# A planned attention and MLP kernel: attention work with new inputs yields to MLP blocks on TensorE, other VectorE durations in the planner, another order at the start

## The chip, the core and the metric

The kernel runs on one NeuronCore of a Trainium2 chip. The time is that of one execution in device microseconds. The engines are TensorE (PE, its weight loads PEld), VectorE (DVE), ScalarE (ACT), GpSimd (POOL) and SyncE (SP), which issues all the DMAs here. Each engine works through its own queue in the order in which the program was written. An instruction whose inputs are not there yet holds up everything behind it on that engine.

## The reference: what is computed

Three layers follow each other. The first is a linear attention with complex decays per channel over 768 positions, for 4 batches of 8 heads of 48 channels. The second is an MLP with a squared ReLU (384 to 2048 to 384) over the 3072 tokens. The third is a gated MLP with an RMS norm before it (384 to 1536 to 384).

```python
def _attn_ref(q, k, v, a_re, a_im):
    mag = np.sqrt(a_re * a_re + a_im * a_im)
    scale = np.minimum(mag, 0.999) / (mag + 1e-06)
    a_re_n, a_im_n = (a_re * scale, a_im * scale)
    for t in range(S):
        S_re, S_im = ar * S_re - ai * S_im + k[t] v[t]^T, ar * S_im + ai * S_re
        y[:, :, t] = np.einsum('bhd,bhde->bhe', q[:, :, t], S_re)

def _moe_ref(x, w_in, w_out):
    r = np.maximum(x @ w_in, 0.0)
    return r * r @ w_out

def _moe2_ref(x, w_gate, w_val, w_out, rms_g):
    xn = x / np.sqrt(np.mean(x * x, axis=-1, keepdims=True) + 1e-06) * rms_g
    g = xn @ w_gate
    return g * (1.0 / (1.0 + np.exp(-g))) * (xn @ w_val) @ w_out
```

## The kernel before

**Tiles.** The tokens are cut into 24 units of 128 (`u`). Two units make a group `g` or pair `p` (12 of them). Matrix products are made of float32 operands split into a high and a low part, so that one product is three passes.

**Attention of a pair.** `chain(p)` runs on VectorE for the most part: `norm` scales the decays; seven `step`s (three instructions each, L274 `XY`, L279, L281) multiply them up within eight positions; `tot` (L290) turns the totals on TensorE and ScalarE copies them to `TP`; four `plevel`s (L313 to L323) scan over them on VectorE; `back` (L339) turns the result back on TensorE; L351 to L355 apply it, and `inv` (L390 to L394) makes the inverse for the keys. Then for each unit `prod` (L402) makes `KP` and `QP` on VectorE; `dtr` (L428, tile `dps`) turns them on TensorE, in halves; `score` (L441, `sps`) multiplies them, in halves; `yy` (L460 and L464, `yps`) makes the output; `state` (L478, `ups`) makes the new state, which GpSimd multiplies with the decay (L488 to L494). `turned` takes the keys through a DRAM tile by two DMAs. `fix` moves rows by six small DMAs, and `split_x` (L703, L705) splits the unit's output into `xs`.

**MLP of a group.** When both units' `xs` are there, 16 pairs of blocks follow: `mlp_h` (L781, nine matmuls) and, two blocks later, `mlp_x` (L806, six matmuls). Between them ScalarE makes three passes and VectorE one (L795, `gs`). The first MLP's 16 weight tiles are converted at the start by `convert` (L507 to L515 and L703/L727, and `lo` on TensorE, L732 and L733), those of the second MLP when attention is over (`set_flag`, `open2`).

**What sets the order.** `Plan` writes the whole program. Every piece of work is a job, a generator of `Op`s with an engine, a duration (`dve(n)` or `act(n)` from the number of elements, or a constant), what it needs and which buffers it takes. `Plan.run` keeps a time for each engine. Over and over it finds, for each engine, the jobs that can start within 0.02 us of the earliest possible planned start there, and takes of those the one with the lowest priority number. Then it emits that instruction. A job's number comes from its group: pair `g` has `F1 * (g - 2)`, the first two pairs `CHAIN0` and `CHAIN1`, products and later steps of a unit 8 and 12 more than their pair, conversion of tile `f` `CONV + f`, MLP blocks `16 * g + f - 60`. On TensorE an MLP block has 120 more (`MLP_PE`, the field `p` of its `Op`). So attention goes before MLP blocks there, whenever it can start in the plan's time.

The part that chooses is

```python
            for c in best.values():
                s0 = min(x[0] for x in c)
                pick.append(min((x for x in c if x[0] <= s0 + 0.02), key=lambda x: x[1:3]))
            s, _, _, j = min(pick, key=lambda x: x[:3])
```

Of the kernel before, what the change touches and what calls it, by code (L numbers as in the profile page):

```python
# [54 lines left out]
class Plan:  # L55
# [35 lines left out]
    def run(self):  # L91
        live = list(self.jobs)
        while live:
            best = {}
            for j in live:
                if j[3] is None:
                    if not all(n in self.t for n in j[5]):
                        continue
                    j[3] = next(j[2])
                if not all(n in self.t for n in j[3].need):  # L100
                    continue
                r = self.ready(j)
# [35 lines left out]
class Attention:  # L138
# [86 lines left out]
    def sumsq(self, m, s, ab, view=lambda t: t, **more):  # L225

        nc = self.nc
        for t, x in zip((m, s), ab):
            yield Op("act", act(768), free=t is s)
            nc.scalar.activation(out=view(t), in_=x, func=AF.Square)  # L230
        yield Op("dve", dve(768))
        nc.vector.tensor_tensor(out=m, in0=m, in1=s, op=ALU.add)
# [3 lines left out]
    def norm(self, p):  # L236
# [15 lines left out]
        yield Op("dve", dve(768))  # L252
        nc.vector.tensor_tensor(out=m, in0=m, in1=r, op=ALU.mult)
        yield Op("dve", dve(768))
# [3 lines left out]
        yield Op("dve", dve(768))  # L258
        nc.vector.scalar_tensor_tensor(out=m, in0=y, scalar=-2.0 / 0.999, in1=r, op0=ALU.max, op1=ALU.mult)
        d = m.rearrange("p (u j d) -> p j u d", u=2, j=8)  # L260
        for c, x in enumerate(self.raw.pop(p)):
            yield Op("dve", dve(768), rel=["raw"] + ["tmp"] * c)
            nc.vector.tensor_tensor(
# [4 lines left out]
    def step(self, p, j):  # L268

        nc = self.nc  # L270
        v, w = self.A[p % 2][:, :, j], self.A[p % 2][:, :, j - 1]
        yield Op("dve", dve(384))
        T = self.sb.tile([128, 2, 2, 2 * D], F32, tag="XY", name="XY", bufs=1)
# [3 lines left out]
        )  # L277
        yield Op("dve", dve(96))
        nc.vector.tensor_tensor(out=v[:, 0], in0=T[:, 0, 0], in1=T[:, 1, 1], op=ALU.subtract)  # L279
        yield Op("dve", dve(96))  # L280
        nc.vector.tensor_tensor(out=v[:, 1], in0=T[:, 0, 1], in1=T[:, 1, 0], op=ALU.add)  # L281
# [15 lines left out]
    def plevel(self, l):  # L297
# [5 lines left out]
        for t, c in ((X, 0), (Y, 1)):  # L303
# [6 lines left out]
            else:  # L310
                for e in range(2):
                    yield Op("dve", 0.14)
                    nc.vector.tensor_tensor(  # L313
# [8 lines left out]
        yield Op("dve", 0.15, done=("TP", self.at) if l == 3 else None)  # L322
        nc.vector.tensor_tensor(out=V[:, 1, :, s:], in0=X[:, 1], in1=Y[:, 0], op=ALU.add)  # L323

    def chain(self, p):
# [23 lines left out]
        for n, (o, i0, i1) in enumerate(((x, a[1], f[1]), (y, a[0], f[1]), (a[0], a[0], f[0]), (a[1], a[1], f[0]))):  # L349
            yield Op("dve", dve(768), rel=["tb"] if n == 3 else [])  # L350
            nc.vector.tensor_tensor(out=o, in0=i0, in1=i1, op=ALU.mult)  # L351
        yield Op("dve", dve(768))
        nc.vector.tensor_tensor(out=a[0], in0=a[0], in1=x, op=ALU.subtract)
        yield Op("dve", dve(768), rel=["tmp", "tmp"], done=("P", p))
        nc.vector.tensor_tensor(out=a[1], in0=a[1], in1=y, op=ALU.add)  # L355
# [18 lines left out]
    def inv(self, p):  # L374
# [12 lines left out]
        nc.scalar.activation(out=z, in_=z, func=AF.Square)  # L387
        yield Op("dve", dve(768), need=[("kin", p)])
        k = self.kin[p].rearrange("p u j d -> p (u j d)")
        nc.vector.tensor_tensor(out=m, in0=m, in1=z, op=ALU.mult)  # L390
        yield Op("dve", dve(768))
        nc.vector.tensor_tensor(out=k, in0=k, in1=z, op=ALU.mult)
        yield Op("dve", dve(768), rel=["tmp", "tmp"], done=("inv", p))
        nc.vector.scalar_tensor_tensor(out=k, in0=m, scalar=2.0, in1=k, op0=ALU.subtract, op1=ALU.mult)  # L394
# [703 lines left out]
```

## Time and profile before

| what | value |
|---|---|
| time, median of 3 runs | 1186.84 us (1186.57 to 1186.89) |
| the profiled execution's own time | 1188.43 us |
| its span, first to last instruction | 1186.7 us |
| PE busy | 1094.6 us (92%) |
| DVE, ACT, POOL busy | 708.8, 666.0, 152.3 us |
| mean granted clock of TensorE | 0.972 |
| share of PE in the chain that ended last | 70%, DVE 18%, ACT 5%, issue 4% |

Two stretches are to be told apart. Until about 714 us attention and the first MLP share the engines. From there to the end the second MLP runs, with its weights converted in the first 50 us of it. The profile's 40 slices show PE at 90% or more in nearly all slices from the fifth on, with single slices of 8 tenths until about 560 us, and a granted clock below one in some slices until about 480 us. A window view gives each engine's busy time in a stretch, and a wait view says on what an engine's idle time ended.

### The profile page before, as it was taken

To read this page: it belongs to the slowest core of one execution; us is meant where nothing else is said; L and a number is where in the kernel's file an instruction comes from. 1 tells how busy PE (TensorE), PEld (TensorE's weight loads), DVE (VectorE), ACT (ScalarE), POOL (GpSimd) and SP (SyncE) were. 2 spreads that over 40 slices of the span, in tenths; PEclk is the share of its full clock that TensorE was granted. 3 is DMA by queue.
4 is the path that set the end of the run, shared out by engine and by line. 5 is a ranking of instruction groups with operands and counts; after the bars stand their busy time and mean duration, and the time that the engine had idled before them with its cause. 6 is when DMAs were issued, how large, how long until landed. Compare 5 with 4: busy or idle time off the path is not lost.

```text
span 1186.7 us, 20383 instructions
## 1 busy us (share of the span) xinstructions
PE 1094.6 (92%) x7874; PEld 1048.0 (88%) x7874; DVE 708.8 (60%) x1419; ACT 666.0 (56%) x1396; POOL 152.3 (13%) x169
## 2 busy tenths in 40 slices
PE   2567989998989998999999999999999999999997
PEld 1245879998979987998999998899999999999997
DVE  4978988888878999988321579732323232222222
ACT  4657877885857886686675786442424242222221
POOL 1124123113120322122000013100000000000000
PEclk9678999998989999999999999999999999999999
DMA  6822324423414324221010294010101010000000
GB/s 187 330 58 75 96 63 123 114 76 104 117 31 116 99 64 132 74 74 44 15 32 16 96 331 161 1 41 1 41 1 40 1 41 1 20 1 20 1 21 23
DMA packets 61339, 85.45 MB, mean 72 GB/s; under 512 B 27440, under 2 KB 54320, under 8 KB 61232
## 3 DMA queue, kind: packets, MB, share of 16 engines
q1 hardware_dynamic: 61232, 84.04, 22.6%
q8 instruction: 64, 1.05, 0.4%
q14 instruction: 43, 0.35, 0.1%
HBM read 64.23 MB, written 18.61 MB: 70 GB/s over the span
## 4 chain that ended last, share of the span: by engine, by line
PE 70%; DVE 18%; ACT 5%; issue 4%; DMA 1%; SPq 1%; POOL 0%; DVEq 0%; ACTq 0%; POOLq 0%
PE h L781 12%; PE o L1002 12%; PE g L966 12%; PE v L966 12%; PE x L806 11%; DVE XY L274 3%; PE sps L441 2%; PE dps L428 2%; DVE ws L513 2%; PE yps L460 1%; DVE cr L515 1%; DMA ws<-in_w 1%; DVE A L279 1%; PE ups L478 1%; PE yps L464 1%
## 5 line engine op out<-in xcount | busy, mean ns | idle before, releaser
L781 PE MATMUL h<-xs,w 128*128 128x256 f32 x1728 | 247.2, 289 | 1.6 <-ACT xs L703 1.0
L806 PE MATMUL x<-w,gs 128*128 128x384 f32 x1152 | 240.5, 344 | 2.4 <-DVE gs L795 1.3
L781 PEld LDWEIGHTS h<-xs,w 128*128 128x128 f32 x1728 | 229.1, 192 | 4.4 <-issue 1.5
L806 PEld LDWEIGHTS x<-w,gs 128*128 128x128 f32 x1152 | 195.5, 191 | 4.5 <-DVE gs L795 1.9
L988 DVE TENSOR_TENSOR uu<-t,v 128x384 f32<-128x384 f32 x96 | 53.1, 553 | 228.7 <-PE v L966 228.4
L1002 PE MATMUL o<-w,us 128*128 128x384 f32 x864 | 168.0, 337 | 4.4 <-DVE us L705 3.4
L966 PE MATMUL g<-ys,w 128*128 128x384 f32 x864 | 166.7, 337 | 0.0
L966 PE MATMUL v<-ys,w 128*128 128x384 f32 x864 | 166.2, 337 | 0.0
L1002 PEld LDWEIGHTS o<-w,us 128*128 128x128 f32 x864 | 150.7, 188 | 7.2 <-DVE us L705 5.5
L966 PEld LDWEIGHTS g<-ys,w 128*128 128x128 f32 x864 | 151.6, 188 | 0.0
L966 PEld LDWEIGHTS v<-ys,w 128*128 128x128 f32 x864 | 150.9, 188 | 0.0
L795 DVE TENSOR_TENSOR gs<-h,gs 128x256 fp32r<-128x256 f32 x192 | 80.3, 418 | 94.1 <-ACT h L793 91.9
L979 ACT ACTIVATE t<-g 128x384 f32<-128x384 f32 x96 | 47.1, 491 | 154.0 <-PE g L966 153.9
L703 ACT CAST us<-uu 128x384 fp32r<-128x384 f32 x96 | 49.1, 511 | 128.0 <-DVE uu L988 128.0
L788 ACT ACTIVATE r<-h 128x256 f32<-128x256 f32 x192 | 73.4, 382 | 73.1 <-PE h L781 72.2
L791 ACT ACTIVATE gs<-r 128x256 fp32r<-128x256 f32 x192 | 80.3, 418 | 6.1
L705 DVE TENSOR_TENSOR us<-uu,us 128x384 fp32r<-128x384 f32 x96 | 54.1, 564 | 46.1 <-ACT us L703 46.1
L793 ACT ACTIVATE h<-r 128x256 f32<-128x256 f32 x192 | 71.2, 371 | 0.0
L446 POOL TENSOR_SCALAR_AFFINE_SELECT st<-st 128x512 f32<-128x512 f32 x48 | 35.0, 738 | 265.0 <-ACT st L444 264.4
L732 PE MATMUL lo<-cr,ident 128*128 128x384 f32 x64 | 37.1, 670 | 27.2 <-DVE cr L515 27.2
L430 ACT COPY dq<-dps 112x512 f32<-112x512 f32 x48 | 52.2, 1120 | 11.9 <-PE dps L428 11.9
L509 POOL TENSOR_SCALAR ws<-ws 128x768 f32<-128x768 f32 x34 | 36.5, 1076 | 166.4 <-ACT cr L507 142.8
(117 smaller groups left out, 1468.2 us busy)
## 6 DMA issues: line engine op xcount, KB each, us to landing
ws<-in_w SPq DMA_DIRECT2D x34, 768.0 KB, 7.1
kb<-KP SPq DMA_DIRECT2D x20, 448.0 KB, 4.1
kt<-kb SPq DMA_DIRECT2D x20, 448.0 KB, 3.9
raw<-in_a_re SPq DMA_DIRECT2D x24, 192.0 KB, 3.3
kin<-in_k SPq DMA_DIRECT2D x24, 192.0 KB, 3.9
qin<-in_q SPq DMA_DIRECT2D x24, 192.0 KB, 3.9
raw<-in_a_im SPq DMA_DIRECT2D x24, 192.0 KB, 4.1
V<-in_v SPq DMA_DIRECT2D x24, 192.0 KB, 2.6
```

The lines of the kernel that those rows point to most:

```text
L430: nc.scalar.copy(out=o[:, half * 4:half * 4 + 4], in_=P.rearrange("p j (b h) -> p j b h", h=H))
L703: nc.scalar.copy(out=hi, in_=src)
L705: nc.vector.tensor_tensor(out=lo, in0=src, in1=hi.bitcast(F32), op=ALU.subtract)
L781: nc.tensor.matmul(hp, lhsT=part(f, 0, a)[:, kk * 128:(kk + 1) * 128], rhs=xs[:, bb, kk, :], start=(i == 0), stop=(i == 8),)
L788: nc.scalar.activation(out=r, in_=hp, func=AF.Relu)
L791: nc.scalar.activation(out=gs[:, 0], in_=r, func=AF.Square)
L793: nc.scalar.activation(out=hp, in_=r, func=AF.Square)
L795: nc.vector.tensor_tensor(out=gs[:, 1], in0=hp, in1=gs[:, 0].bitcast(F32), op=ALU.subtract)
L806: nc.tensor.matmul(x_ps[g][i], lhsT=gs[:, a, i * CH:(i + 1) * CH], rhs=part(f, 1, bb), start=(f == 0 and n == 0), stop=(f == F1 - 1 and n ...
L966: nc.tensor.matmul(P, lhsT=part(T_GATE + f, half, a)[:, kk * 128:(kk + 1) * 128], rhs=ys[:, bb, kk, :], start=(i == 0), stop=(i == 8),)
L988: nc.vector.tensor_tensor(out=uu, in0=t_t.pop((g, f)), in1=P, op=ALU.mult)
L1002: nc.tensor.matmul(o_ps[g][i], lhsT=us[:, a, i * CH:(i + 1) * CH], rhs=part(T_OUT2 + f // 2, f % 2, bb), start=(f == 0 and n == 0), stop=( ...
```

## The change

The planner is changed in three places. No instruction's operands or shapes change, and the program has as many instructions of each kind as before.

```diff
-CHAIN0, CHAIN1, CONV, CONV_D, WHOLD = -300, -16, -100, 1, 4
+CHAIN0, CHAIN1, CONV, CONV_D, WHOLD = -300, -6, -12, 1, 4
+LATE = {"pe": 2.0}
+def dve2(n):
+    return 0.11 + 0.00116 * n
...
-                    best.setdefault(j[3].eng, []).append((max(r, self.free.get(j[3].eng, 0.0)), j[0] + j[3].p, j[1], j))
+                    s = max(r, self.free.get(j[3].eng, 0.0))
+                    fresh = r + LATE.get(j[3].eng, 0.0) * (j[3].p == 0.0)
+                    best.setdefault(j[3].eng, []).append((s, j[0] + j[3].p, j[1], j, fresh))
...
-                pick.append(min((x for x in c if x[0] <= s0 + 0.02), key=lambda x: x[1:3]))
-            s, _, _, j = min(pick, key=lambda x: x[:3])
+                now = [x for x in c if x[0] <= s0 + 0.02]
+                old = [x for x in now if x[4] <= s0]
+                pick.append(min(old, key=lambda x: x[1:3]) if old else min(now, key=lambda x: (x[4], *x[1:3])))
+            s, _, _, j, _ = min(pick, key=lambda x: x[:3])
...
-        yield Op("dve", dve(384))
+        yield Op("dve", dve2(384))
...
-            yield Op("dve", 0.21)
+            yield Op("dve", 0.27)
-        yield Op("dve", 0.15)
+        yield Op("dve", 0.24)
```

**Attention yields.** On TensorE a job that is no MLP block (its `p` is 0) counts as old only when its inputs have been ready in the plan for 2.0 us; an MLP block is old as soon as it is ready. Of the old ones the lowest number still goes first. Only if none is old is the one taken that comes of age first. Nothing is delayed by it if no MLP block is ready.

**Durations.** The VectorE steps of attention (`norm`, `step`, `plevel`, the application in `chain`, `inv`) are planned with `dve2(n)` and larger constants: 1.00 us instead of 0.87 for 768 elements, 0.56 instead of 0.47 for 384, 0.22 instead of 0.18 for 96; in `plevel` 0.27, 0.20 and 0.24 instead of 0.21, 0.14 and 0.15. `prod`, the conversions and the MLP keep `dve(n)`.

**The beginning.** The numbers of the first group's MLP are -60 to -45 on ScalarE and VectorE. Conversions had -100 to -85 and have -12 to 3 now, and the second pair has -6 instead of -16; its products have 2 to 6, behind the third pair's chain, which has 0.

The order on the engines shows the following. In the middle of the first stretch, around the tenth pair's `tot` on TensorE (`h` and `x` are MLP blocks, the rest is attention), there stood before

```order
L428 MATMUL dps<-ident,KP_90 112x128 x4
L781 MATMUL h<-xs,w 128x256 x9
L428 MATMUL dps<-ident,QP 112x128 x4
L806 MATMUL x_5199<-w,gs 128x384 x3
L806 MATMUL x_5200<-w,gs 128x384 x3
L428 MATMUL dps<-ident,QP 112x128 x4
L290 MATMUL tot<-ident,A_87 48x128 x4
L781 MATMUL h<-xs,w 128x256 x9
L441 MATMUL sps<-dq,dk 128x128 x8
```

and now there stands

```order
L300 MATMUL tot<-ident,A_87 48x128 x4
L816 MATMUL x_5084<-w,gs 128x384 x3
L816 MATMUL x_5085<-w,gs 128x384 x3
L791 MATMUL h<-xs,w 128x256 x9
L816 MATMUL x_5084<-w,gs 128x384 x3
L816 MATMUL x_5085<-w,gs 128x384 x3
L451 MATMUL sps<-dq,dk 128x128 x4
L791 MATMUL h<-xs,w 128x256 x9
```

The steps of attention stand further apart, with MLP blocks between them, and the two halves of `sps` no longer follow each other.

On VectorE near the start, the second pair (`A_87`) gave its products before the third pair (`A_86` again) was normed; there stood before

```order
L394 SCALAR_TENSOR_TENSOR kin<-m,kin 128x768
L795 TENSOR_TENSOR gs<-h,gs 128x256
L402 TENSOR_TENSOR KP_90<-A_87,kin 128x8x48 x2
L402 TENSOR_TENSOR KP_91<-A_87,kin 128x8x48
L795 TENSOR_TENSOR gs<-h,gs 128x256
L402 TENSOR_TENSOR KP_91<-A_87,kin 128x8x48
L402 TENSOR_TENSOR QP<-A_87,qin 128x8x48 x2
L259 SCALAR_TENSOR_TENSOR m<-A_86 128x768
L795 TENSOR_TENSOR gs<-h,gs 128x256
L263 TENSOR_TENSOR A_86<-raw,m 128x768 x2
L274 TENSOR_TENSOR XY<-A_86 128x384
```

and now, after the whole of the third pair's steps and scan,

```order
L331 TENSOR_TENSOR TP<-pX,pY 112x64
L333 TENSOR_TENSOR TP<-pX,pY 112x64
L412 TENSOR_TENSOR KP_91<-A_87,kin 128x8x48 x2
L412 TENSOR_TENSOR QP<-A_87,qin 128x8x48 x2
L361 TENSOR_TENSOR x<-A_86,back 128x768
L805 TENSOR_TENSOR gs<-h,gs 128x256
L361 TENSOR_TENSOR x<-A_86,back 128x768
L361 TENSOR_TENSOR A_86<-A_86,back 128x768
```

The products of the second pair's second unit (`KP_91`, `QP`) have moved behind the third pair's scan.

On TensorE, at the seam from the first group's MLP to the second's (the 17th `h`), there stood before

```order
L806 MATMUL x_796<-w,gs 128x384 x3
L806 MATMUL x_797<-w,gs 128x384 x3
L781 MATMUL h<-xs,w 128x256 x9
L428 MATMUL dps<-ident,QP 112x128 x4
L781 MATMUL h<-xs,w 128x256 x18
L428 MATMUL dps<-ident,QP 112x128 x4
```

and now there stands ahead of the 17th `h`

```order
L438 MATMUL dps<-ident,QP 112x128 x4
L816 MATMUL x_752<-w,gs 128x384 x3
L816 MATMUL x_753<-w,gs 128x384 x3
L451 MATMUL sps<-dq,dk 128x128 x8
L438 MATMUL dps<-ident,KP_90 112x128 x8
L470 MATMUL yps<-st,V_89 64x128 x8
L438 MATMUL dps<-ident,QP 112x128 x8
L451 MATMUL sps<-dq,dk 128x128 x4
```

followed by `ups`, the other half of `sps` and both halves of the sixth unit's `dps` and then three `h`: attention of the next pair has moved ahead of the second group's first MLP block.

## Rows read from the trace of the kernel before

**Rows 1.** Windows: us, busy PE, PEld, DVE, ACT, POOL, then PEclk, DMA share, GB/s

```profile
0.00:95.00 95.00, 45.93 (x208) 28.59 (x208) 69.80 (x128) 53.42 (x89) 16.15 (x23) 0.80 0.56 191
95.00:165.00 70.00, 63.73 (x484) 56.21 (x483) 62.63 (x127) 53.79 (x116) 22.43 (x24) 0.93 0.27 77
165.00:560.00 395.00, 369.37 (x3337) 353.45 (x3338) 342.48 (x735) 296.81 (x636) 86.47 (x95) 0.98 0.31 88
560.00:714.00 154.00, 154.00 (x1191) 151.93 (x1190) 65.28 (x141) 111.48 (x269) 15.24 (x17) 1.00 0.29 101
714.00:765.00 51.00, 46.58 (x256) 44.06 (x256) 49.29 (x60) 29.43 (x47) 11.99 (x11) 1.00 0.21 79
```

**Rows 2.** What PE waited for from 165 to 560 us: us, times, longest

```profile
PE tot L290 <- DVE A L279: 14.4, 8, 3.6
PE back L339 <- DVE TP L321: 4.1, 3, 2.3
```

**Rows 3.** Windows after 165 us with a lowered clock, columns as in rows 1

```profile
282.10:288.95 6.85, 6.85 (x39) 6.85 (x39) 3.54 (x15) 3.22 (x8) 0.63 (x1) 0.65 0.50 146
333.30:336.80 3.50, 3.50 (x45) 3.20 (x44) 0.72 (x2) 3.24 (x7) 0.00 (x0) 0.80 0.00 0
463.00:466.40 3.40, 3.40 (x35) 3.15 (x35) 3.13 (x12) 2.75 (x6) 1.10 (x2) 0.80 0.24 82
```

**Rows 4.** PE in order of time, at the sixth tot: start, us, what, idle before

```profile
280.60 1.26 PE L290 MATMUL tot<-ident,A 128*48 128x128 f32 x8 [3.58 <-DVE A L279]
281.80 2.29 PE L781 MATMUL h<-xs,w 128*128 128x256 f32 x9
```

**Rows 5.** DVE and POOL in order of time: steps alone, and beside GpSimd

```profile
32.20 0.56 DVE L274 TENSOR_TENSOR XY<-A 128x384 f32<-128x384 f32 x1
32.80 0.26 DVE L279 TENSOR_TENSOR A<-XY 128x96 f32<-128x96 f32 x1
33.26 0.56 DVE L274 TENSOR_TENSOR XY<-A 128x384 f32<-128x384 f32 x1
...
76.36 0.94 DVE L279 TENSOR_TENSOR A<-XY 128x96 f32<-128x96 f32 x1
...
76.30 1.76 POOL L509 TENSOR_SCALAR ws<-ws 128x768 f32<-128x768 f32 x2 [6.52 <-ACT cr L507]
```

**Rows 6.** PE in order of time: MLP blocks alone, and beside attention

```profile
573.26 1.23 PE L781 MATMUL h<-xs,w 128*128 128x256 f32 x9
574.33 1.21 PE L806 MATMUL x<-w,gs 128*128 128x384 f32 x6
...
594.29 1.34 PE L781 MATMUL h<-xs,w 128*128 128x256 f32 x9
595.48 0.60 PE L428 MATMUL dps<-ident,QP 128*112 128x128 f32 x4
...
599.53 1.95 PE L441 MATMUL sps<-dq,dk 112*128 112x128 f32 x16
```

**Rows 7.** The first two groups' last xs on DVE, the 17th h on PE

```profile
95.09 0.55 DVE L705 TENSOR_TENSOR xs<-xt,xs 128x384 fp32r<-128x384 f32 x1
...
164.24 0.55 DVE L705 TENSOR_TENSOR xs<-xt,xs 128x384 fp32r<-128x384 f32 x1
...
164.85 0.98 PE L781 MATMUL h<-xs,w 128*128 128x256 f32 x6 [0.49 <-DVE xs L705]
```

**Rows 8.** What DVE waited for until 170 us

```profile
DVE xs L705 <- ACT xs L703: 5.1, 1, 5.1
DVE pX L319 <- ACT TP L295: 2.8, 1, 2.8
```

**Rows 9.** DVE groups by shape: busy us, mean ns of one

```profile
L274 DVE TENSOR_TENSOR XY<-A 128x384 f32<-128x384 f32 x84 | 50.1, 596 | 2.5
L402 DVE TENSOR_TENSOR KP<-A,kin 128x384 f32<-128x384 f32 x48 | 26.0, 581 | 0.1
L390 DVE TENSOR_TENSOR m<-m,z 128x768 f32<-128x768 f32 x12 | 12.1, 1009 | 10.9 <-ACT z L387 10.9
```

More of the change, by code (lines that the diff above doesn't have):

```diff
@@ L230, in sumsq @@
             nc.scalar.activation(out=view(t), in_=x, func=AF.Square)
-        yield Op("dve", dve(768))
+        yield Op("dve", dve2(768))
         nc.vector.tensor_tensor(out=m, in0=m, in1=s, op=ALU.add)
@@ L251, in norm @@
         nc.scalar.activation(out=r, in_=y, func=AF.Square, accum_out=self.ss[:, 0, p:p + 1])
-        yield Op("dve", dve(768))
+        yield Op("dve", dve2(768))
         nc.vector.tensor_tensor(out=m, in0=m, in1=r, op=ALU.mult)
-        yield Op("dve", dve(768))
+        yield Op("dve", dve2(768))
         nc.vector.scalar_tensor_tensor(out=y, in0=m, scalar=3.0, in1=y, op0=ALU.subtract, op1=ALU.mult)
@@ L257, in norm @@
         nc.scalar.activation(out=r, in_=y, func=AF.Copy, scale=-0.24975e-6, bias=-0.4995)
-        yield Op("dve", dve(768))
+        yield Op("dve", dve2(768))
         nc.vector.scalar_tensor_tensor(out=m, in0=y, scalar=-2.0 / 0.999, in1=r, op0=ALU.max, op1=ALU.mult)
@@ L261, in norm @@
         for c, x in enumerate(self.raw.pop(p)):
-            yield Op("dve", dve(768), rel=["raw"] + ["tmp"] * c)
+            yield Op("dve", dve2(768), rel=["raw"] + ["tmp"] * c)
             nc.vector.tensor_tensor(
@@ L277, in step @@
         )
-        yield Op("dve", dve(96))
+        yield Op("dve", dve2(96))
         nc.vector.tensor_tensor(out=v[:, 0], in0=T[:, 0, 0], in1=T[:, 1, 1], op=ALU.subtract)
-        yield Op("dve", dve(96))
+        yield Op("dve", dve2(96))
         nc.vector.tensor_tensor(out=v[:, 1], in0=T[:, 0, 1], in1=T[:, 1, 0], op=ALU.add)
@@ L311, in plevel @@
                 for e in range(2):
-                    yield Op("dve", 0.14)
+                    yield Op("dve", 0.2)
                     nc.vector.tensor_tensor(
@@ L317, in plevel @@
                 continue
-            yield Op("dve", 0.21)
+            yield Op("dve", 0.27)
             nc.vector.tensor_tensor(out=o, in0=i0, in1=i1, op=ALU.mult)
-        yield Op("dve", 0.15)
+        yield Op("dve", 0.24)
         nc.vector.tensor_tensor(out=V[:, 0, :, s:], in0=X[:, 0], in1=Y[:, 1], op=ALU.subtract)
-        yield Op("dve", 0.15, done=("TP", self.at) if l == 3 else None)
+        yield Op("dve", 0.24, done=("TP", self.at) if l == 3 else None)
         nc.vector.tensor_tensor(out=V[:, 1, :, s:], in0=X[:, 1], in1=Y[:, 0], op=ALU.add)
@@ L349, in chain @@
         for n, (o, i0, i1) in enumerate(((x, a[1], f[1]), (y, a[0], f[1]), (a[0], a[0], f[0]), (a[1], a[1], f[0]))):
-            yield Op("dve", dve(768), rel=["tb"] if n == 3 else [])
+            yield Op("dve", dve2(768), rel=["tb"] if n == 3 else [])
             nc.vector.tensor_tensor(out=o, in0=i0, in1=i1, op=ALU.mult)
-        yield Op("dve", dve(768))
+        yield Op("dve", dve2(768))
         nc.vector.tensor_tensor(out=a[0], in0=a[0], in1=x, op=ALU.subtract)
-        yield Op("dve", dve(768), rel=["tmp", "tmp"], done=("P", p))
+        yield Op("dve", dve2(768), rel=["tmp", "tmp"], done=("P", p))
         nc.vector.tensor_tensor(out=a[1], in0=a[1], in1=y, op=ALU.add)
@@ L387, in inv @@
         nc.scalar.activation(out=z, in_=z, func=AF.Square)
-        yield Op("dve", dve(768), need=[("kin", p)])
+        yield Op("dve", dve2(768), need=[("kin", p)])
         k = self.kin[p].rearrange("p u j d -> p (u j d)")
         nc.vector.tensor_tensor(out=m, in0=m, in1=z, op=ALU.mult)
-        yield Op("dve", dve(768))
+        yield Op("dve", dve2(768))
         nc.vector.tensor_tensor(out=k, in0=k, in1=z, op=ALU.mult)
-        yield Op("dve", dve(768), rel=["tmp", "tmp"], done=("inv", p))
+        yield Op("dve", dve2(768), rel=["tmp", "tmp"], done=("inv", p))
         nc.vector.scalar_tensor_tensor(out=k, in0=m, scalar=2.0, in1=k, op0=ALU.subtract, op1=ALU.mult)
```

## The prediction

> **What bounds the kernel now.** I read the windows by stretch first [rows 1]. From 560 to 714 us PE is busy all the time at a clock of 1.00, and after 765 us it is PE alone that works, back to back. So PE's work sets the end, and a microsecond in which it stands still, or runs at half its clock, is lost for good as long as the work behind it is still there to be done. Such microseconds lie in three places.
>
> Until 165 us PE is busy 45.9 + 63.7 of 165 us [rows 1], so 55.3 us are idle. There VectorE is the limit: in the window from 95 us it is busy 62.6 of 70 us, with the 16 weight conversions and the first pairs' chains on it. From 165 to 560 us PE is idle 395 - 369.4 = 25.6 us. The waits there are of one kind: 14.4 us in eight waits for `tot`, whose input is the last `step`, and 4.1 us in three for `back`, whose input is the scan [rows 2]; nothing else reaches 2.5 us. From 714 to 765 us PE is idle 4.4 us, while VectorE is busy 49.3 of 51 with the second MLP's weights.
>
> These waits in the middle come from planned durations that are too short. A `step` takes 1.06 us from one `XY` to the next [rows 5]; the plan has 0.47 + 2 x 0.18 = 0.82, seven times per pair. So the planner believes that the chain is done 1.7 us earlier than it is, puts `tot` there, and PE stands in front of it although MLP blocks are ready right behind. After such a wait the clock is granted at half, too: `tot` waits 3.58 us at 280.6, and the `h` behind it takes 2.29 us instead of 1.23 [rows 4, 6]. There are four such stretches after 165 us (three in [rows 3], the fourth like the last two), in all 17.1 us, and PE was busy in all of them, so they cost half of the time at half the clock. The mean clock of 0.65 in 6.85 us is 4.8 us at 1.2 GHz as the window cuts it, 0.80 in 3.4 us is 1.4 us; the `h` at 288 us still runs at half, so I take the stretches whole: 17.1 / 2 = 8.5 us as a bound from above, 4.5 from below. What the middle loses is thus 25.6 + 8 = about 34 us.
>
> **The change part by part.**
>
> *Attention yields, and longer durations.* Both do the same thing: `tot`, `back` and the other attention steps go later into PE's queue, behind MLP blocks that need nothing. The order shows it: from the 17th `h` to the end of the first MLP the attention steps stand in 147 separate places instead of 122. With `dve2` a step is planned at 0.56 + 2 x 0.22 = 1.00 us against 1.06, so the plan misses a pair's seven steps by 0.4 us instead of 1.7; the scan, planned at 4.6 us, is now longer than its instructions are without disturbance. And 2 us of margin lie on top. So a wait that was 3.6 us at most [rows 4] is covered by about 1.3 + 2 us in the plan. I take 5 us of the 34 as what remains (bounds: 2, if only the seams stay, and 17, if half of it does).
>
> The trace has one thing that no linear duration holds. The `A` instruction of 96 elements at L279 takes 0.26 us, and 0.94 us at 76.36, while a GpSimd instruction ran from 76.30 on [rows 5]. GpSimd is busy 86.5 of the 395 us [rows 1], so such a step falls beside it about one time in five, and loses up to 0.7 us each time: 21 instructions a pair x 0.22 x 0.7 = 3.2 us at most for a pair's steps, against 2.4 us of margin. That is why 17 is the bound and not 5. The Trainium skill (SBUF — State Buffer, Who interferes with whom) says that a VectorE instruction with two SBUF inputs and a GpSimd instruction that reads SBUF exclude each other for the whole length of the first. The row at 76.36 agrees with it. By that rule alone the waits would stay wherever GpSimd falls on a chain, which is the rival below.
>
> *What separating costs.* An `h` alone takes 1.07 us to the next block, an `h` in front of a `dps` 1.19 [rows 6]. Twenty-five more places at 0.12 us are 3 us. All of it is on the path, since PE is the path (bounds 0 and 6).
>
> *The beginning.* This is where I expect a loss. The second group's 17th `h` waits for its last `xs`, at 164.24 before, and PE was there just in time: it waited 0.49 us [rows 7]. In the new order of VectorE 29 more instructions stand ahead of that `xs`, because the third pair's chain has number 0 and the second pair's products have 2 and more. They are eight of 768 elements (about 1.0 us each), two writes of `A` (the same), seven products (0.58), four `XY` (0.60) and eleven small ones (0.3 to 0.55, taken together 4.6): 8 + 2.2 + 4.1 + 2.4 + 2.7 = 19.3 us of records [rows 9, 5]. Records overlap: from 95.09 to 164.24 us [rows 7] the same kind of sum gives 68 us, where VectorE was busy some 62 of 69 us [rows 1]. So 19.3 us are about 17.8 us of time. Against that, 5.1 us of waiting for the first group's `xs` [rows 8] can go, as `xs` of the first unit now stands inside the scan; but the copy behind the ninth conversion now waits for `ups`, which stands behind that conversion's `lo` on PE. I take 3 us of gain from it (bounds 0 and 5), so the second group starts 15 us later. PE does more in that time: ahead of the 17th `h` stand six more halves of `dps` (0.35 us from start to the next block), two more of `sps` (0.86, half of 1.71), and one `ups` (an estimate from the `sps` row, about 1 us): 2.1 + 1.7 + 1 = 5 us that need not be done later [rows 6]. Net +10 us, with bounds of +4 and +16. The other queues follow: SP has the rows of `fix` for the first unit ahead of the key transfer, as before, and the conversions' loads were issued by 41 us already; neither adds a wait that I can price above 1 us.
>
> *The seam to the second MLP.* `set_flag` stands behind 175 `h` blocks instead of 168, so the loads that depend on it come about 7 x 2.1 = 15 us later against the first `g`. But the loads of the first 16 tiles wait for the last group's own `x` blocks in both orders, which have not moved against `g`. What moves into the stretch in which VectorE is full are some turned inputs: two of six `t` now stand behind the first `g`. I put it at 0, with bounds of -3 and +4; if its cover were gone it would add to the 4.4 us that PE is idle there [rows 1].
>
> *After 765 us* nothing changes but the place of three `t` per group: 0.
>
> **Sum.** Against the span of 1186.7 us: -34 + 5 + 3 + 10 + 0 = -16 us, so 1170.7 us. The profiled execution took 1188.43 us in all and the median of the runs is 1186.84, close to the span, so I take the same 16 us from the median: **1171 us**. A measurement of this kernel can tell about 0.2% (2.4 us) from no change, so 1184.5 to 1189.2 us counts as the same.
>
> **Rivals.**
>
> *The beginning is free.* The third pair's work that stands ahead of the second group is done in VectorE's gaps (6.5 us of waits in 95 to 165 us, [rows 1, 8]) and the new waits do not arise. Then the beginning costs +1 and the middle keeps 2 to 5: -34 + 3 + 3 + 1 = -27, **1160 us**. For it: the first `h` has 9 conversions ahead of it instead of 10. Against it: VectorE is nearly full there, and 29 instructions are counted, not guessed.
>
> *GpSimd breaks the plan.* Steps are held up in bursts, and half of the middle's loss stays, at `tot`, `back` or at `dps`: -34 + 17 + 3 + 10 = -4, at most with the milder beginning -10: about **1180 us**. For it: rows 5. Against it: with more MLP blocks per pair (15 of them between two `tot` now, 13 before) VectorE has more time per pair and runs ahead of the plan.
>
> *Slower: the first group's blocks run out.* At the seam PE has done 16 of 16 blocks, and its 17th `h` needs both `xs`. PE's queue there has `yps` of the fourth unit behind `dps` of the fifth, so it waits for the third pair's inverse as well, and `xs` waits for ScalarE, six DMAs and VectorE in turn. If each of these adds its wait (3 us at ScalarE, as at `pX`, 5 us as at `xs`, [rows 8]) to the upper bound of 16, the beginning costs 24, PE comes out of it at half the clock (2 to 3 us), and with 17 us left in the middle the sum is -34 + 17 + 3 + 26 = +12: **1199 us**. It decides from the point where the 17th `h` starts later than about 195 us with half of the waits for `tot` still there.
>
> *The change does not do what it says.* Margin acts only where an MLP block is ready at the same planned moment; if the old waits were not due to the order, the time stays within 0.2%. The 147 places against 122 speak against it.
>
> **How the numbers follow.** Forecast (1164 to 1176) 0.45; free beginning (1154 to 1164) 0.25; GpSimd (1176 to 1184) 0.15; no effect 0.05; slower 0.10. Faster by over 0.2%: 0.45 + 0.25 + 0.15 = 0.85; same 0.05; slower 0.10. The range of 1157 to 1183 leaves out some 0.03 below and 0.16 above.
>
> **What would show it.** In the new profile the windows from the 17th `h` to 560 us should have PE idle under 8 us, waits for `tot` and `back` together under 4 us, and no more than one stretch of half the clock. The second group's last `xs` should start at 175 to 183 us; at 165 the first rival is right, beyond 195 the slower one. The stretch behind the first `g` should have PE idle 2 to 8 us in 50. I am wrong if `tot` still waits over 10 us, or if waits of the same size appear at `yps`, `ups` or `h` in the middle.

## The result, and the profile after

The changed kernel takes 1164.87 us (median of 4 runs, 1164.41 to 1165.43). Against the runs of the kernel before beside it (median 1186.70 us) the ratio is 0.9822, with an interval of 0.9805 to 0.9839: some 21 us faster. The profiled execution took 1165.43 us with a span of 1163.4 us, against 1186.7. The forecast was 1171 with a range of 1157 to 1183; the sign and the range hold, and the size is 6 us short. In the sum the beginning together with the separation is 9 us too dear, and the seam to the second MLP is 4.5 us too cheap.

The windows of the changed kernel by stretch, columns as in [rows 1]; lines of code have moved by ten (L290 is L300 now):

```profile
0.00:95.00 95.00, 50.03 (x231) 34.86 (x231) 77.98 (x156) 59.03 (x103) 19.33 (x26) 0.87 0.58 201
95.00:165.00 70.00, 61.71 (x473) 53.19 (x472) 65.54 (x111) 55.96 (x112) 24.85 (x21) 0.97 0.29 81
165.00:560.00 395.00, 390.75 (x3527) 375.51 (x3526) 341.86 (x721) 306.64 (x668) 101.21 (x96) 0.99 0.31 87
560.00:686.00 126.00, 125.83 (x984) 123.19 (x983) 59.57 (x122) 89.50 (x207) 14.44 (x15) 1.00 0.32 114
686.00:737.00 51.00, 45.20 (x249) 41.83 (x247) 50.61 (x68) 37.98 (x66) 12.21 (x11) 1.00 0.24 90
```

From 165 to 560 us PE was idle for 25.6 us; now it is 4.25 us, and all of that lies before 177 us, when the second group's blocks begin. What PE waited for from 165 to 560 us (engine line waited for, us, times, longest), the answer to [rows 2]:

```profile
PE h L791 <- DVE xs L715: 2.2, 1, 2.2
PE sps L451 <- ACT dq L440: 1.2, 1, 1.2
PE h L791 <- ACT xs L713: 0.7, 1, 0.7
PE dps L438 <- ACT st L454: 0.2, 1, 0.2
```

There is no row of `tot` or `back` left. The stretches of [rows 3] are gone; one of 3.4 us at half the clock remains behind the seam of the groups (the first line), and in the 383 us from 177 us on PE has no idle time at all (the second):

```profile
177.90:181.30 3.40, 3.40 (x19) 3.18 (x19) 2.64 (x8) 1.99 (x6) 0.00 (x0) 0.50 0.02 8
...
177.00:560.00 383.00, 383.00 (x3465) 369.18 (x3465) 332.43 (x703) 301.73 (x661) 98.22 (x92) 1.00 0.30 84
```

PE in order of time at the sixth `tot`, the answer to [rows 4]. It waits for nothing, and the `h` behind it takes 1.33 us instead of 2.29:

```profile
276.68 1.13 PE L488 MATMUL ups<-V,kt 128*64 128x48 f32 x32
277.64 0.64 PE L300 MATMUL tot<-ident,A 128*48 128x128 f32 x8
278.22 1.33 PE L791 MATMUL h<-xs,w 128*128 128x256 f32 x9
```

The second group's last `xs` on DVE and its first blocks on PE, the answer to [rows 7]. It comes 11.9 us later than before (164.24 us), and PE waits for it 2.17 us instead of 0.49:

```profile
176.10 0.56 DVE L715 TENSOR_TENSOR xs<-xt,xs 128x384 fp32r<-128x384 f32 x1
...
173.93 0.61 PE L791 MATMUL h<-xs,w 128*128 128x256 f32 x3 [0.67 <-ACT xs L713]
176.72 4.59 PE L791 MATMUL h<-xs,w 128*128 128x256 f32 x24 [2.17 <-DVE xs L715]
```

For all kernels I now cut the span at two events instead of fixed times: the start of the second group's last `xs` ("xs") and the first `g` ("g"). First the kernel before, up to xs, from xs to g, and 70 us from g:

```profile
0.00:164.20 164.20, 109.35 (x689) 84.65 (x689) 131.62 (x252) 106.41 (x203) 38.58 (x47) 0.85 0.43 142
164.20:714.20 550.00, 523.88 (x4530) 505.73 (x4529) 408.77 (x877) 409.29 (x905) 101.81 (x112) 0.98 0.31 92
714.20:784.20 70.00, 65.58 (x369) 62.95 (x369) 56.26 (x72) 35.62 (x59) 11.89 (x11) 1.00 0.18 65
```

and the changed kernel:

```profile
0.00:176.10 176.10, 119.20 (x761) 94.10 (x761) 152.09 (x281) 119.90 (x219) 47.17 (x51) 0.90 0.47 152
176.10:686.40 510.30, 509.51 (x4449) 493.05 (x4450) 393.26 (x826) 391.63 (x868) 112.66 (x107) 1.00 0.31 92
686.40:756.40 70.00, 62.43 (x348) 58.70 (x347) 59.92 (x87) 44.41 (x77) 12.21 (x11) 1.00 0.17 63
```

The second length minus its first number is PE's idle time: 54.9, 26.1 and 4.4 us before; 56.9, 0.8 and 7.6 us after. So the middle gave back nearly all its idle time, the later xs brought only 2 us more of it, and the stretch behind g became worse.

### The profile page after: what moved, and what is told of

Its sections match the earlier page's. It is cut to its first block, busy times and chain, and to the rows that moved or that the text cites. A ratio compares the mean times of both kernels' runs of the same rounds, so it can differ in the third digit from the quotient of the medians.

```text
span 1163.4 us, 20341 instructions
## 1 busy us (share of the span) xinstructions
PE 1091.6 (94%) x7874; PEld 1045.1 (90%) x7874; DVE 721.3 (62%) x1419; ACT 673.3 (58%) x1400; POOL 172.0 (15%) x169
## 4 chain that ended last, share of the span: by engine, by line
PE 81%; DVE 11%; ACT 2%; issue 2%; DMA 1%; SPq 1%; POOL 0%; DVEq 0%; ACTq 0%; POOLq 0%
PE h L791 17%; PE x L816 16%; PE o L1012 12%; PE v L976 12%; PE g L976 12%; PE sps L451 4%; PE dps L438 3%; DVE ws L523 2%; PE yps L470 2%; PE ups L488 2%; PE yps L474 2%; DVE cr L525 1%; DVE XY L284 1%; DMA ws<-in_w 1%; PE lo L742 1%
## 5 line engine op out<-in xcount | busy, mean ns | idle before, releaser
L791 PEld LDWEIGHTS h<-xs,w 128*128 128x128 f32 x1728 | 225.8, 191 | 12.7 <-DVE gs L805 4.8
L456 POOL TENSOR_SCALAR_AFFINE_SELECT st<-st 128x512 f32<-128x512 f32 x48 | 38.8, 809 | 234.4 <-ACT st L454 234.2
L451 PE MATMUL sps<-dq,dk 112*128 112x128 f32 x384 | 55.2, 292 | 4.5 <-ACT dq L440 3.2
L498 POOL TENSOR_TENSOR Y<-W,pe 48x384 f32<-48x384 f32 x40 | 47.6, 1190 | 74.3 <-DVE W L494 58.3
```

The lines of the kernel that those rows point to most:

```text
L451: nc.tensor.matmul(P[:, i], lhsT=K[:, h, :], rhs=Q[:, h, :], start=True, stop=True)
L791: nc.tensor.matmul(hp, lhsT=part(f, 0, a)[:, kk * 128:(kk + 1) * 128], rhs=xs[:, bb, kk, :], start=(i == 0), stop=(i == 8),)
```

## The experiments

The last five columns hold for each kernel's profiled execution: PE's idle time up to xs and from xs to g (windows as above), the time before g in which PE was busy while the granted clock was 0.5, the time from `flagp` (the matmul of `set_flag`) to g, and from g to the end. "Y" is yielding, "D" the longer durations, "B" the new beginning; a dash is the state before.

| kernel | Y D B | ratio to before, interval | idle to xs | idle xs to g | half clock | flag to g | g to end |
|---|---|---|---|---|---|---|---|
| before | - - - | 1 | 54.9 | 26.1 | 50.3 | 54.0 | 472.5 |
| changed | Y D B | 0.9822 (0.9805 to 0.9839) | 56.9 | 0.8 | 30.3 | 38.2 | 477.0 |
| late_only | Y - - | 0.9934 (0.9918 to 0.9951) | 64.5 | 10.0 | 39.9 | 40.0 | 475.0 |
| dur_only | - D - | 0.9822 (0.9806 to 0.9839) | 60.5 | 9.6 | 32.3 | 54.0 | 473.1 |
| start_only | - - B | 0.9976 (0.9962 to 0.9990) | 62.0 | 19.4 | 44.6 | 54.0 | 472.0 |
| late_dur | Y D - | 0.9864 (0.9848 to 0.9881) | 62.6 | 4.7 | 24.1 | 38.4 | 476.7 |
| dur_start | - D B | 0.9743 (0.9715 to 0.9771) | 53.5 | 6.3 | 18.0 | 54.0 | 471.9 |
| turn_free | Y but `t` | 0.9821 (0.9793 to 0.9849) | 57.5 | 0.7 | 42.0 | 38.4 | 476.4 |
| chain1_old | Y D half | 0.9904 (0.9873 to 0.9934) | 66.5 | 1.0 | 32.3 | 32.9 | 483.6 |
| conv_old | Y D half | 0.9936 (0.9915 to 0.9957) | 61.2 | 5.3 | 30.4 | 29.7 | 484.3 |
| end_free | Y to 130th h | 0.9780 (0.9764 to 0.9797) | 56.9 | 0.7 | 27.3 | 54.0 | 472.4 |
| beg_free | Y from 16th h | 0.9800 (0.9784 to 0.9816) | 55.7 | 4.5 | 29.4 | 38.3 | 477.0 |
| mid_late32 | Y 32nd to 130th | 0.9800 (0.9784 to 0.9817) | 55.0 | 8.5 | 30.6 | 54.0 | 473.4 |
| dur_108 | - D+8% B | 0.9738 (0.9725 to 0.9751) | 54.0 | 4.7 | 23.4 | 54.0 | 472.0 |

The time of g less the two idle times and half of the half-clock time is 606 to 614 us in all of them. That is PE's work at full clock before g. The bookkeeping thus closes to about 4 us, and what is smaller than that between two kernels it can't settle by itself. Nor does half clock ahead of xs cost its half: the changed kernel and `turn_free` have the same order until 662 us and 26.9 and 38.6 us of it there, and xs comes at 176.1 and 176.9 us.

### Which part gives the gain

Alone the longer durations (`dur_only`), alone the yielding (`late_only`), alone the beginning (`start_only`), and all but the beginning (`late_dur`). Each takes its lines back from the changed kernel:

```diff
 # dur_only, dur_start: no yielding
-                pick.append(min(old, key=lambda x: x[1:3]) if old else min(now, key=lambda x: (x[4], *x[1:3])))
+                pick.append(min(now, key=lambda x: x[1:3]))
 # late_only, start_only: durations as before (and the constants of plevel)
-    return 0.11 + 0.00116 * n
+    return 0.075 + 0.00104 * n
 # late_only, dur_only, late_dur: beginning as before
-CHAIN0, CHAIN1, CONV, CONV_D, WHOLD = -300, -6, -12, 1, 4
+CHAIN0, CHAIN1, CONV, CONV_D, WHOLD = -300, -16, -100, 1, 4
```

`dur_only`, what was expected:

> The longer VectorE durations alone; TensorE picks as before and the first numbers are the old ones. Theory A (the middle's loss comes from durations planned too short, and either remedy removes it): waits of PE between 165 and 560 us fall from 25.6 to under 8 us, the seam stays as before, 1160 us (1154 to 1168). Theory B (only the yielding does it, since without it nothing puts an MLP block ahead of attention): 1180 to 1187 us, waits for tot and back still over 12 us.

Measured: 1167.42 us, 0.9822. The durations alone give the ratio that the whole change gives. The time lies in the band of the first theory, 7 us above its middle. Its windows up to xs and from xs to g show PE idle for 9.6 us instead of 26.1 in the second:

```profile
0.00:165.90 165.90, 105.39 (x689) 82.16 (x689) 134.36 (x252) 109.41 (x205) 39.35 (x47) 0.88 0.43 143
165.90:692.20 526.30, 516.73 (x4528) 500.82 (x4528) 411.24 (x878) 407.55 (x902) 97.73 (x112) 0.99 0.32 96
```

From 165 to 600 us `tot` still waits 3.7 us in four waits and `back` 2.7 us in three. So 10 us of the waits for `tot` went with a longer plan alone. The theory that expected 1180 us and more falls. The other expected PE idle under 8 us from 165 to 560 us, and it is 10.0, so the durations alone don't remove all of it.

`late_only`, what was expected:

> The yielding alone; old durations, old first numbers. Theory A: idle of PE in the middle under 8 us, seam 4 us dearer, 1162 us (1156 to 1170). Theory B: the same, 1162 us. Theory C (the margin of 2 us does not cover an error of 1.7 us a pair plus the scan's, so both remedies are needed): 1172 to 1180 us, waits for back and tot of 8 to 15 us.

Measured: 1180.26 us, 0.9934, at the edge of the band of the theory that needed both parts. But that theory expected 8 to 15 us of waits for `tot` and `back`, and from xs on they come to 3.1 us. These waits shrink here too, and others take their place. The two largest of PE from 176.5 us to the first `g`:

```profile
PE x L816 <- DVE x L825: 6.2, 4, 2.5
PE tot L300 <- DVE A L289: 2.8, 3, 2.0
```

`x` at L825 is the copy that takes a group's first-MLP output out of PSUM on VectorE, so the first `x` of the next group waits for it. With VectorE planned too short its queue runs behind the plan, the copies too, while the margin covers only PE's attention steps. `late_dur` bears that out: it differs by the longer durations alone, and there this wait is 0.3 us in one.

`start_only`, what was expected:

> The other first numbers alone. Theory A (the other beginning costs some 7 us net): the middle's 34 us stay, 1190 us (1186 to 1198). Rival (the beginning is itself a gain, hidden by the new order of the middle): 1170 to 1183 us.

Measured: 1185.02 us over ten runs that spread from 1182.39 to 1190.58, ratio 0.9976. It is neither the loss that my own theory expected nor the gain of its rival: alone the beginning brings 0.1 to 0.4%. The profiled execution was the slowest of the ten (1190.58 us), so its row of the table is that of a long one.

`late_dur`, what was expected:

> Yielding and durations with the old first numbers, so the beginning alone is undone. Theory A: 7 us faster than the changed kernel, 1158 us (1154 to 1163), and the second group's last xs at 165 to 172 us. Rival (the other beginning is a gain or free): 1165 us or more.

Measured: 1171.89 us, 0.9864. With the beginning undone the kernel is slower by 5 us by the ratios (7 by the medians), not faster. Up to xs PE is idle 62.6 us instead of 56.9, although xs comes at 172.1, that is 4 us earlier than in the changed kernel, and from xs to g 4.7 instead of 0.8.

### Yielding undone, and which number of the beginning counts

`dur_start` keeps the durations and the beginning. What was expected:

> Yielding undone; longer durations and the new beginning kept. Theory A (the three parts act on different stretches: the new beginning takes 4 to 7 us off, as it does from late_dur to after and from before to start_only, and leaves the middle alone): 1167.4 - 4 to 7 = 1160 to 1163 us, with PE idle 7 to 11 us from the second group's last xs to the first g, and the first group of the second MLP at 64 to 65 us instead of 68. That would beat the changed kernel. Theory B (the new beginning needs yielding, since its attention steps come late and would be waited for): 1167 to 1173 us, with waits for tot and back of 5 us or more between 165 and 600 us.

Measured: 1156.32 us, ratio 0.9743 (0.9715 to 0.9771). This beats the changed kernel by 9 us by the ratios. Theory B falls. Theory A has the direction, but the time is 4 us below its band and PE's idle time from xs to g, 6.3 us, is below its 7 to 11. Nor do the parts simply add up, as it held: the beginning gains 3 us alone (`start_only`), 5 with yielding and the durations, and 9 with the durations alone. The windows:

```profile
0.00:165.70 165.70, 112.17 (x713) 86.33 (x714) 142.13 (x266) 116.04 (x215) 45.57 (x44) 0.93 0.43 143
165.70:682.10 516.40, 510.15 (x4506) 494.81 (x4505) 401.20 (x864) 399.10 (x892) 101.03 (x116) 1.00 0.32 97
682.10:752.10 70.00, 65.52 (x369) 62.89 (x369) 56.26 (x72) 35.64 (x59) 11.92 (x11) 1.00 0.17 64
```

The middle is idle for 6.3 us, more than with yielding. But up to xs 7 us less are lost than in `dur_only`, no stretch of half clock is left between xs and g, and the 70 us behind g read as they did before the change (65.52 us busy there, 62.43 in the changed kernel).

For `chain1_old` and `conv_old` one number each is put back in the changed kernel:

```diff
-CHAIN0, CHAIN1, CONV, CONV_D, WHOLD = -300, -6, -12, 1, 4
+CHAIN0, CHAIN1, CONV, CONV_D, WHOLD = -300, -16, -12, 1, 4     # chain1_old
+CHAIN0, CHAIN1, CONV, CONV_D, WHOLD = -300, -6, -100, 1, 4     # conv_old
```

> The changed kernel with the second pair's number back at -16; conversions stay at -12. Theory A (the gain of the new beginning, 7 us against undoing both numbers, comes from the first group's MLP going ahead of the later conversions): stays at 1164 to 1166 us. Theory B (it comes from the second pair's products standing behind the third pair's chain, so that the chains are ahead of PE when the second group starts): 1170 to 1172 us, with waits of attention steps on PE in the 60 us behind the second group's start as in late_dur.

> The changed kernel with the conversions back at -100; the second pair stays at -6. Theory A (the gain comes from the conversions' number): 1170 to 1172 us, with the first h at 93 to 97 us instead of 88. Theory B (it comes from the second pair's number): 1164 to 1166 us although the first h is as late as in the kernel before.

Measured: 1177.16 and 1179.88 us. Both are slower than the changed kernel, and slower than `late_dur` with neither number. So the gain belongs to neither alone; both theories of both runs fall, and the pair must be looked at as one order. `chain1_old` holds a lesson of its own. Its windows:

```profile
0.00:160.90 160.90, 94.42 (x605) 75.11 (x605) 129.18 (x246) 99.80 (x184) 45.09 (x45) 0.86 0.44 145
160.90:691.70 530.80, 529.75 (x4603) 511.34 (x4604) 409.19 (x861) 410.18 (x904) 114.47 (x111) 1.00 0.31 94
691.70:761.70 70.00, 60.78 (x307) 56.22 (x307) 60.97 (x84) 43.80 (x74) 14.22 (x14) 0.93 0.18 69
```

Its xs is the earliest of all kernels, at 160.9 us, and yet PE has been idle the longest until then, 66.5 us. The second group was ready while the first group's weights were not: a `lo` of the conversions still stands on PE at 182.26 us. The date of xs alone is no measure of the beginning; it has to be read with the work that stands ahead of it.

### Where the stretch behind the first g lost its time

The changed kernel needs 477.0 us from g to the end, 4.5 more than before. What PE waited for in the 70 us behind g:

```profile
PE o L1012 <- DVE us L715: 3.7, 5, 1.1
PE g L976 <- DVE w L715: 1.6, 1, 1.6
PE v L976 <- DVE uu L998: 1.1, 1, 1.1
PE g L976 <- ACT t L989: 1.0, 1, 1.0
```

`g <- w` is a wait for a converted weight, which was not there before. `turn_free` exempts the turned inputs from yielding, `end_free` ends all yielding at the 130th `h`:

```diff
 # turn_free
-        yield Op("pe", 0.34, acq=["gv"] + ([] if kk else ["ys"]), rel=["xr"] if kk == KT - 1 else [])
+        yield Op("pe", 0.34, acq=["gv"] + ([] if kk else ["ys"]), rel=["xr"] if kk == KT - 1 else [], p=0.001)
 # end_free (nh counts the h that are planned; the lines that count it, and the one that then takes from all in `now`, left out)
-                    fresh = r + LATE.get(j[3].eng, 0.0) * (j[3].p == 0.0)
+                    fresh = r + LATE.get(j[3].eng, 0.0) * (j[3].p == 0.0 and 0 <= self.nh < 130)
```

> The changed kernel, but the turned inputs (t) of the second MLP are exempt from yielding; all six stand ahead of the first g again. Theory A (the 4 us that the seam lost come from the two t that moved behind the first g): first group of the second MLP at 64 to 65 us instead of 68, time 1161 to 1162.5 us. Theory B (the seam lost them because the flag that opens the second MLP's weights comes later, after 175 h instead of 168): first group stays at 67 to 69 us, time 1164 to 1166 us.

Measured: 1165.76 us. All six `t` stand ahead of g again, and nothing is gained: 476.4 us from g to the end. That theory falls.

> The changed kernel, but attention stops yielding after the 130th h of the first MLP; the flag stands behind 168 h again instead of 175. Theory A (the 4 us of the seam come from the later flag, which opens the second MLP's weights): first group of the second MLP at 64 to 65 us instead of 68, 472 to 473 us from the first g to the end, PE idle under 3 us between the second group's last xs and the first g, time 1159.5 to 1162 us. Theory B (the seam lost them by something else, such as VectorE's work left over): first group 67 to 69 us, time 1164 to 1166 us.

Measured: 1162.33 us, 0.9780 (0.9764 to 0.9797), and its interval lies wholly below that of the changed kernel. The 70 us behind g:

```profile
684.80:754.80 70.00, 65.52 (x370) 62.88 (x369) 56.27 (x72) 35.67 (x59) 11.93 (x11) 1.00 0.17 64
```

65.52 us busy and 472.4 us to the end, as the theory of the flag asked for; the time is 0.3 us above its band. Its profiled execution took 1159.28 us where its other runs took 1162.12 to 1163.07, so its columns up to g may flatter it by 3 us: its xs comes 1.8 us before that of the changed kernel, though VectorE's order is the same in both until 521 us.

`flagp` on PE in three kernels (matmuls, ns at least, median and at most, first and last start), first before (g at 714.2):

```profile
L890 PE MATMUL flagp<-ident,t x2: 270/270/271, 660.2 to 660.3; 128*1 128x128 f32 x2
```

changed (g at 686.4):

```profile
L900 PE MATMUL flagp<-ident,t x2: 272/272/272, 648.2 to 648.3; 128*1 128x128 f32 x2
```

and `end_free` (g at 684.8):

```profile
L900 PE MATMUL flagp<-ident,t x2: 270/270/271, 630.8 to 630.9; 128*1 128x128 f32 x2
```

Over all kernels the time from g to the end follows the lead of the flag: 54.0 us of lead give 471.9 to 473.4 us, 40.0 give 475.0, 38.2 to 38.4 give 476.4 to 477.0, 32.9 give 483.6, and 29.7 give 484.3. The last two have 9.7 and 12.1 us of half clock behind g in that. The second MLP's weights can be converted only once the flag is set: the first conversion on VectorE starts 39.1 us ahead of g before and in `end_free`, and 24.1 us ahead in the changed kernel, and the last one ends 49.7, 49.7 and 58.1 us behind g. VectorE is full there (50.6 of 51 us), so PE waits for part of what the lead loses: its idle time behind g rose from 11.2 to 14.2 us. No run moves the flag alone, for `end_free` changes the whole order behind the 130th `h`.

### Is yielding worth it in the middle alone

Both keep the durations and the beginning; the condition on `nh` is `16 <= self.nh` in `beg_free` and `32 <= self.nh < 130` in `mid_late32`.

> The changed kernel, but attention yields only from the 16th h of the first MLP on, that is from the end of the first group. Theory A (yielding at the beginning, where VectorE and not PE is the limit, is what puts the second group's last xs at 176 us instead of the 166 us of the kernel without yielding): last xs at 164 to 168 us, PE idle plus half of its half-clock time until then 6 us less than in the changed kernel, first group of the second MLP still at 67 to 69 us, time 1157 to 1161 us. Theory B (the lateness is in the order of VectorE, set by the two numbers): last xs at 174 to 178 us, time 1164 to 1166 us.

> The changed kernel with yielding only between the 32nd and the 130th h, neither at the beginning nor at the end of attention. Theory A (yielding costs 6 us at the beginning and 4 us at the seam, and gains the 6 us of idle time that the kernel without yielding has in the middle): first group 64 to 65 us, last xs 164 to 168 us, PE idle 0 to 3 us between it and the first g, time 1150 to 1154 us, faster than all others. Theory B (with the longer durations the margin has nothing left to gain): 1155 to 1158 us, as without yielding.

Measured: 1164.77 and 1165.18 us. In `beg_free` xs comes 6.4 us earlier (169.7, 1.7 us behind theory A's band), but the time is that of theory B: PE is idle 1.2 us less up to xs and 3.7 us more behind it. `mid_late32` misses both theories, A by 11 us and B by 7. Its three longest waits from 165 to 600 us:

```profile
PE h L791 <- DVE xs L715: 3.7, 4, 1.2
PE tot L300 <- DVE A L289: 2.4, 2, 1.6
PE dps L438 <- ACT dq L440: 0.9, 2, 0.7
```

The next group's `h` waits for `xs` four times here, and `dur_start` has no such row. That attention which yields delivers its `xs` later is my reading of it; it isn't shown, for the changed kernel yields all the way and has one such wait for VectorE. Of the 9.0 us between the spans of the two, 1.0 lie up to xs, where all engines have the same order in both. 6.5 lie between xs and g, 2.2 of them idle time and 0.9 half clock; the rest is PE's work, and why it takes longer stays open. 1.5 lie behind g, where a stretch of 3.4 us at half the clock falls. That 28.9 us of half clock stand ahead of xs in the one and 18.0 in the other brought that 1.0 us at most.

### What is left of the waits

`dur_108` is `dur_start` with VectorE's other work planned 8% longer from the 32nd to the 150th `h`:

```diff
-            cost = op.cost
+            cost = op.cost * (1.08 if op.eng == "dve" and op.p == 0.0 and 32 <= self.nh < 150 else 1.0)
```

> Yielding undone; longer durations and new beginning kept, as in the kernel that is the fastest so far (1156.3 us, 6.3 us of PE idle between the second group's last xs and the first g, no half clock there). In addition VectorE's work outside the MLP is planned 8% longer between the 32nd and the 150th h: a step at 1.08 us where the trace has 1.06. Order at the beginning and the flag (behind 168 h) are unchanged. Theory A (what is left of the waits is what the plan is still short by): PE idle 0 to 3 us in that stretch, time 1151 to 1154 us. Theory B (what is left comes from single steps held up, or from ScalarE, so that a longer plan only moves attention later): idle 4 to 9 us with waits of h for xs among them, time 1155 to 1160 us.

Measured: 1155.65 us, 0.9738 (0.9725 to 0.9751), the same as `dur_start` within the intervals. Time and idle time (4.7 us) lie in the bands of theory B, but the waits of `h` for `xs` that it named are not there. What PE waited for from 165 to 600 us (the two longest):

```profile
PE tot L300 <- DVE A L289: 3.8, 5, 0.8
PE sps L451 <- ACT dk L440: 0.4, 2, 0.2
```

No wait is longer than 0.8 us now, where [rows 2] have 3.6. What remains is of the size of one step held up beside GpSimd (0.26 against 0.94 us, [rows 5]). The trace speaks for it: ahead of each of the five waits for `tot`, 8 to 10 of the chain's 21 `step` instructions ran beside a GpSimd instruction, and the 21 took 2.8 to 3.1 us more than alone. But three chains as long in the same stretch were not waited for, and no run takes GpSimd's work away, so it is not shown.

## Why the prediction came out as it did

The terms of the sum against what the profiled executions show, with half of the half-clock time behind xs counted as lost:

| term | predicted | measured |
|---|---|---|
| middle: -34 and +5 left | -29 | 25.3 of idle time and 6.6 of half clock: -31.9 |
| beginning | +10 (4 to 16) | xs 11.9 later, 7.8 less of PE's work behind it: +4.1 |
| separation | +3 (0 to 6) | contained in the 7.8 |
| seam to the second MLP | 0 (-3 to +4) | +4.5 |
| sum | -16 | -23.3 |

The 7.8 us are PE's busy time from xs to g, each less half of its half clock: 523.88 - 8.25 = 515.6 us before and 509.51 - 1.7 = 507.8 us now.

**The middle was right.** The waits were due for the most part to planned durations that are too short, and they took the half clock with them. In `dur_only` the longer durations by themselves take the idle time from 26.1 to 9.6 us and the half clock from 16.5 to 7.8. With yielding and the new beginning the residue was 0.8 us and 3.4 us at half the clock, 2.5 us together instead of 5. One remark of it was wrong: the `h` at 288 us did not run at half, it took 1.31 us. The windows of [rows 3] lie 2 us behind the stretches themselves, as the first of them shows:

```profile
280.10:286.90 6.80, 6.30 (x29) 5.94 (x30) 3.01 (x10) 2.25 (x6) 0.33 (x1) 0.50 0.50 146
```

PE was busy in 16.5 of the 17.1 us, and the bound of 8.5 us stands. And "both do the same thing" is too simple: yielding alone leaves VectorE's queue behind the plan, so it moves waits from `tot` to the copies (`late_only`).

The rival of GpSimd fell. By the rule of the Trainium skill that I cited for it (SBUF — State Buffer, Who interferes with whom) steps should be held up wherever GpSimd falls on a chain. The rows agree that they are (0.94 us in [rows 5], and 1.25 us for a product in the last section), but 1.0 us per step in the plan and the margin together were enough to hide it: no wait for `tot` is left in the changed kernel. The sum set 2.4 us of margin against it; with 0.4 us that the plan still misses, 2 us leave 1.6.

**The beginning is the step that failed.** I counted 29 instructions ahead of the second group's last xs, and the windows have 281 instead of 252 on VectorE. (My list of them names 32; the small ones are eight, not eleven.) They brought 20.5 us more of VectorE's busy time (131.62 to 152.09), near the 19.3 of the sum. But xs came 11.9 us later and not 15: VectorE's idle time up to it fell by 8.6 us (32.6 to 24.0), where I had taken off 4.5. And 7.8 us less of PE's work stood behind xs, where I had 5. So the beginning, with whatever separating costs, came to 4.1 us, and the forecast had 13 for the two.

The date doesn't belong to the new numbers alone either. With them and the longer durations but no yielding xs comes at 165.7 us (`dur_start`), with yielding and the old numbers at 172.1 (`late_dur`). Beside the longer durations the new beginning even gains: 5 us with yielding (ratios 0.9864 in `late_dur`, 0.9822 in the changed kernel) and 9 without (0.9822 in `dur_only`, 0.9743 in `dur_start`). Which order brings that is not known, since neither number does it alone. The price was nearer to that of the first rival, "the beginning is free", whose 1160 us missed by about the seam. Its mechanism held in part: 8.6 us of the new work went into VectorE's gaps, but xs was not at 165 us, as it asked.

**The seam was outside its bounds, for a reason that stood in the text.** I saw that the flag comes about 15 us later against g; it was 15.8 (54.0 to 38.2). I then named as its cover that the loads of the first 16 tiles wait for the last group's `x` anyway. The program has it so for the loads. The conversions wait for the flag and started 15 us later against g, and VectorE has no room to catch up. `end_free`, where the flag has its lead again, gives the 4.5 us back.

**The separation** can't be read. PE's full-clock work before g is 5.5 us more in the changed kernel (608.1 to 613.6 us), of the size I put in, but it scatters by as much between kernels: it is 613.3 us in `dur_start`, where PE's order is not more divided than before, and 608.4 in `turn_free`, which has the changed kernel's order until 662 us.

All signs that I named came in (no wait for `tot`, one stretch of half clock, xs at 176.1, 5.8 us idle in 51 behind g) and still the time was 6 us off: none of them measured how much of PE's work stood ahead of xs. The sign that I had chosen for the first rival, xs at 165, even spoke against it.

**What the change as a whole does.** The longer durations alone give as much as all of it. The beginning adds 9 us to that (`dur_start`). Yielding then takes that away again: of the 9.4 us between the spans of the changed kernel and `dur_start`, 5.1 lie behind g, where the flag has 15.8 us less lead. Before g yielding lets xs come 10.4 us later and makes the stretch from xs to g 6.1 us shorter, 5.5 of it by less idle time. `dur_start` and `dur_108`, without yielding, beat both kernels.

## What to carry to other kernels

Where a planner lays an in-order queue, correct its durations from the trace first; a margin on one engine was no substitute here (0.9934 against 0.9822), and with the durations right it cost 5 to 9 us (0.9822 to 0.9864 with the old beginning, 0.9743 to 0.9822 with the new). A delay at a seam is priced by the date less all of the bound engine's work that then stands ahead of it, and both are to be measured; the date alone says little. When an event moves, list all that waits for it, not only what is loaded, and ask of each whether the engine that does it has room.

## What the runs showed of the hardware

The same work took GpSimd and VectorE longer when it was moved. GpSimd's 169 instructions take 152.3 us before and 172.0 us in the changed kernel, 149.0 in `dur_only` and 179.1 in `beg_free`. The `KP` products at L412 took 581 ns each before [rows 9] and take 710 now:

```profile
L412 DVE TENSOR_TENSOR KP<-A,kin 128x384 f32<-128x384 f32 x48 | 32.1, 710 | 0.3
```

24 of the 48 now run beside a GpSimd instruction, where 5 did before; alone they take 0.55 us in both kernels, beside one 0.87 on average now. Like this one:

```profile
105.16 1.25 DVE L412 TENSOR_TENSOR KP<-A,kin 128x384 f32<-128x384 f32 x1
...
104.39 1.60 POOL L504 TENSOR_TENSOR St<-St,Y 112x384 f32<-112x384 f32 x1
105.96 1.21 POOL L519 TENSOR_SCALAR ws<-ws 128x768 f32<-128x768 f32 x1
```

A plan with one duration per shape doesn't hold that, and its error depends on the order that it makes.

The clock is not set by the order alone. In the changed kernel and in `turn_free` PE and VectorE have the same order until long behind xs. From 20 to 50 us the granted clock was yet 0.91 in the one,

```profile
20.00:50.00 30.00, 13.53 (x36) 8.01 (x36) 28.38 (x61) 15.95 (x30) 4.08 (x4) 0.91 0.80 313
```

and 0.74 in the other, where PE was busy 1.75 us less in that stretch:

```profile
20.00:50.00 30.00, 11.78 (x33) 6.56 (x33) 28.94 (x62) 16.80 (x32) 3.80 (x4) 0.74 0.77 303
```

So the half-clock column of the table, up to xs, holds some microseconds that belong to the single execution and not to the kernel. They cost little there: with 11.7 us more of it `turn_free` reached xs 0.9 us later.
